# A kernel that orders its own program: the cost functions of its planner replaced by the durations of the trace

## The chip, the cores and the metric

One core of one Trainium2 chip runs the kernel as one launch. The metric is the device time in microseconds (us), lower is better; three runs are given for the kernel before. The engines are named as the profile names them: PE (matrix multiply), PEld (its weight load), DVE (vector), ACT (scalar, activation), POOL (GpSimd), SP (its queue issues the DMAs).

## The reference

The inputs are q, k, v of shape (4, 8, 576, 64) in float32, a forget gate f of shape (4, 8, 576), and the weights of two feed-forward layers (512 by 1536, 512 by 1536, 1536 by 512 each).

```python
scores = q @ k^T / 8 + decay            # decay[i, j] = cum[i] - cum[j], cum = cumsum(log f)
attn   = softmax(causal(scores)) @ v    # per batch and head
x      = attn as (2304 tokens, 512)
x      = x / rms(x) * rms_g
x      = (silu(x @ w_gate) * (x @ w_val)) @ w_out      # layer 1, with the norm before it
out    = (silu(x @ w_gate2) * (x @ w_val2)) @ w_out2   # layer 2, without a norm
```

## The kernel before

**Tiling.** The 2304 tokens are worked through in four groups (`GROUPS`): two groups of 2 x 256 tokens (the first 256 of two sequences each), then two groups of 2 x 320 tokens. For every group there is attention over 8 heads of its two sequences, a norm, and two feed-forward layers of 36 weight pieces (128 x 512) each. The work of PE is float32 in two parts: every operand is split into a high part and a low part, and each product takes three matmuls (L1485 to L1487). The last group replaces part of the products by sums and differences of blocks (L1187 to L1189).

**Weights.** They arrive as 64-bit floats. `convert` (from L1406) turns each of the 72 pieces into float32 with a few instructions: a multiplication by a power of two (L1419 on ACT, L1421 on DVE, L1423 on POOL), a shift of one byte column of each word (L1429 on ACT, or L1431 on DVE), a mask (L1435, DVE) and a merge (L1441, DVE); the result is stored (L1445). Then `split` makes the high part (`hi_op`, L284 on ACT or L286 on DVE) and the low part (`lo_op`, L289 on POOL or DVE). This is done once, while the first group is worked on; later groups fetch the stored pieces.

**Who sets the order.** The program is written by a planner that runs when the kernel is built. Each part of the work (a head pair, a weight piece, a norm, a thread of the feed-forward layers) is a generator that asks for operations. The planner keeps a time at which each engine comes free, takes the request that can start first, puts it behind the others of its engine and adds its cost to the engine's time. An operation is ready 0.14 us (`LATENCY`) after the planned end of the operations that it needs. Requests within 0.01 us of each other go by priority. Nothing of this exists on the chip: there each engine runs its instructions in the written order and waits on semaphores.

**Choice of engine.** Where an operation may run on several engines (`either`), the planner takes the smallest sum of planned start, cost and a handicap written by hand. Handicaps depend on the phase (0 until the eighth step of the first group, 1 until the eighth step of the second, then 2, 3, 4). For the byte shift the handicap of DVE is `HAND_LOW = (-0.22, 0, 9, -0.01, 0.08)`. "DVL" stands for a DVE operation that the planner does not let overlap with one of POOL.

**The costs** are the functions at the head of the file: `pe` and `pe4` (matmuls), `dve`, `dve2` (the form at double rate), `act`, `actp` (ACT with its source in PSUM), `pool_`. Each is a slope times the columns plus a constant.

**Fills.** Where the planner sees PE idle in the beginning (until step 12 of the first group's feed-forward work), it writes matmuls on zeros into the program:

```python
    def fill(time):
        for _ in range(int((time - FILL_GAP) / 0.107)):
            nc.tensor.matmul(idle[2][:, :SPLIT], zeros[:, :P], zeros[:, :SPLIT], start=True, stop=True)
```

They are L355 in the profile; 22 further ones at the very start (L364) are written out without the planner. The head pairs of the first half are `pair_queries` (scores L640 and L641, maxima L654, exponentials L662, scaling L680 to L684, transposes L701, values L716), the others `pair_wide` and `wide_part` (exponentials L820, scaling L841 to L845, transposes L893, values L921).

Of the kernel before, what the change touches and what calls it, by code (L numbers as in the profile page):

```python
# [17 lines left out]
B, H, S, D = 4, 8, 576, 64  # L18
# [6 lines left out]
WP = 512  # L25
# [40 lines left out]
HAND_CONV = (0.68, 1, 1.67, 0.2, -0.2)  # L66
STYLE1 = 3
HAND_SCALE = (0.3, 0.2)
HAND_LOW = (-0.22, 0, 9, -0.01, 0.08)
# [140 lines left out]


def pe(n):
    return max(0.107, n / 2400 + 0.0025)


def dve(n):
    return n / 960 + 0.067


def dve2(n):  # L220
    return n / 1920 + 0.067


def act(n):
    return n / 1200 + 0.093


def pool_(n):
    return n * 0.0022 + 0.1


def actp(n):
    return n / 1200 + 0.052


def pe4(n):
    return n / 600 + 0.003


def dma(n):  # L240
# [17 lines left out]
def tile_attention_moe_moe(  # L258
# [17 lines left out]
    plan = Plan()  # L276
# [349 lines left out]
    def pair_queries(hds, before, started, done):  # L626

        hd = hds[0]
        h, s, n = hd.h, hd.s, hd.qn
        tok, _ = yield Take(sc_tokens[0], (before, hd.kq_ready))  # L630
        rows = ((0, P), (P, 2 * P))
        sc, es = [], []
        for x in hds:
            q, k = x.kq[:, 0], x.kq[:, 1]
            bank, e0 = yield Take(banks, ())

            def mm():
                for c, (col, kn) in enumerate(rows):
                    qs = slice(c * P, (c + 1) * P)
                    nc.tensor.matmul(bank[:, col : col + kn], q[:, qs], k[:, :kn], start=c == 0, stop=False)  # L640
                nc.tensor.matmul(  # L641
                    bank[:, : 4 * P].rearrange("p (a n) -> p a n", n=2 * P)[:, :, :P], mir[:, 0], mir[:, 1:3], start=False, stop=True
                )

            e = yield op("PE", pe4(3 * P) + pe(2 * P), mm, hd.kq_ready, e0)
            x.kq_drop(e)
            sc.append(bank)
            es.append(e)
        later(started, e)
        st, e0 = yield Take(hd.slots["tm"], ())  # L650
        for x, (bank, e) in enumerate(zip(sc, es)):
            for c, (col, kn) in enumerate(rows):
                o, i = st[:, 2 * x + c : 2 * x + c + 1], bank[:, col : col + kn]
                em = yield op("DVE", dve(kn), lambda: nc.vector.tensor_reduce(o, i, axis=AX.X, op=ALU.max), e, e0)  # L654
        em = yield op("DVE", dve(4), lambda: nc.vector.tensor_scalar(st[:, 4:8], st[:, 0:4], -0.125, None, op0=ALU.mult), em)
        d, e0 = yield Take(hd.slots["d"], ())
        for x, bank in enumerate(sc):
            for c, (col, kn) in enumerate(rows):
                o, i, j = d[:, x, col : col + kn], bank[:, col : col + kn], 2 * x + c
                e = yield op(  # L660
                    "ACT", actp(kn) + 0.186,
                    lambda: nc.scalar.activation(  # L662
                        o, i, AF.Exp, scale=0.125, bias=st[:, 4 + j : 5 + j], accum_out=st[:, 8 + j : 9 + j]
                    ), em, e0,
                )
            banks.give(bank, e)
        sc_tokens[0].give(tok, e)
        e = yield op("DVE", dve(4), lambda: nc.vector.tensor_scalar(st[:, 8:12], st[:, 8:12], 1e-9, None, op0=ALU.add), e)
        e = yield op("DVE", dve(4) + 0.01, lambda: nc.vector.reciprocal(st[:, 8:12], st[:, 8:12]), e)
        es = []  # L670
        for c, (col, kn) in enumerate(rows):
            o = d[:, :, col : col + kn]

            def scale(en):
                if en == "POOL":
                    m = st[:, 8 + c : 12 : 2].unsqueeze(2).to_broadcast([P, 2, kn])
                    nc.gpsimd.tensor_tensor(o, o, m, op=ALU.mult)
                    return
                for x in range(2):
                    m = st[:, 8 + 2 * x + c : 9 + 2 * x + c]  # L680
                    if en == "ACT":
                        nc.scalar.mul(o[:, x], o[:, x], m)
                    else:
                        nc.vector.tensor_scalar(o[:, x], o[:, x], m, None, op0=ALU.mult)  # L684

            es.append((yield either(
                (
                    ("DVL", 2 * (dve2(kn) + 0.06), 0.0),
                    ("POOL", pool_(2 * kn), HAND_SCALE[0]),
                    ("ACT", 2 * act(kn), HAND_SCALE[1]),  # L690
                ), scale, e,
            )))
        es = Event(max(es[0].t, es[1].t))
        hd.slots["tm"].give(st, es)
        pts = []
        for x in range(2):
            bank, e0 = yield Take(banks, (es,))

            def turn_():
                for i in range(3):  # L700
                    nc.tensor.transpose(bank[:, i * P : (i + 1) * P], d[:, x, i * P : (i + 1) * P], ident)  # L701

            e = yield op("PE", 3 * 0.109, turn_, es, e0)
            ed = e
            pt, e0 = yield Take(hd.slots["p"], ())
            e = yield hi_op(3 * P, pt, bank[:, : 3 * P], e, e0, psum=True)
            banks.give(bank, e)
            pts.append((pt, e))
        hd.slots["d"].give(d, ed)

        bank, e0 = yield Take(banks, (hd.v_ready, *(e for _, e in pts)))
        for x, (pt, e) in enumerate(pts):

            def mm():
                for c in range(2):
                    nc.tensor.matmul(  # L716
                        bank[:, c * P : n], hds[x].v[:, c], pt[:, c * 2 * P : (2 + c) * P],
                        start=(x == c == 0), stop=(x == c == 1),
                    )

            e = yield op("PE", pe4(n) + pe4(P), mm, e, e0)
            hds[x].v_drop(e)
            hd.slots["p"].give(pt, e)
        e = yield hi_op(n, xT[h // 2][s][:, :n], bank[:, :n], e, xT_free[hd.g][s], psum=True)
        banks.give(bank, e)
        for x in done:
            later(x, e)
# [28 lines left out]
    def wide_part(hds, part, st, hl, ev, e0):  # L756
        hd = hds[0]
        kind, s = hd.kind, hd.slots
        joint = part == 2
        kn = ((128, 256), (384, 512, 576))[kind][part]  # L760
# [51 lines left out]
        for i in range(2):  # L812
            if joint:
                o, src, b = dt[:, 512 * i : 512 + D * i], sc[i][:, : (512, D)[i]], 0
            else:
                o, b = dt[:, kn * i : kn * (i + 1)], i
                src = sc[i][:, :kn] if kind else sc[0][:, kn * i : kn * (i + 1)]
            ex.append((yield op(
                "ACT", actp(kn if not joint else (512, D)[i]) + 0.186,
                lambda: nc.scalar.activation(  # L820
                    o, src, AF.Exp, scale=0.125, bias=st[:, c + 2 + b : c + 3 + b], accum_out=st[:, c + 4 + i : c + 5 + i]
                ), em, e1,
            )))
            if kind:
                banks.give(sc[i], ex[i])
# [3 lines left out]
        e = ex[1]  # L829
# [6 lines left out]
        for i in range(k):  # L836
            o, m = dt[:, w // k * i : w // k * (i + 1)], st[:, c + 4 + i : c + 5 + i]

            def scale(en):
                if en == "ACT":  # L840
                    nc.scalar.mul(o, o, m)  # L841
                elif en == "POOL":
                    nc.gpsimd.tensor_scalar(o, o, m, 1.0, op0=ALU.mult, op1=ALU.mult)
                else:
                    nc.vector.tensor_scalar(o, o, m, None, op0=ALU.mult)  # L845

            n = w // k
            es.append((yield either(
                (("POOL", n / 1200 + 0.2, 0.0), ("ACT", act(n) + 0.09, HAND_SCALE[1]), ("DVL", dve(n) + 0.2, HAND_SCALE[0] + 0.5)), scale, e
            )))  # L850
        later(ev["scaled"], Event(max(x.t for x in es)))

# [553 lines left out]
    def convert(i):  # L1406
# [8 lines left out]
        high = x[:, :, 1]  # L1415

        et = yield either(
            (("ACT", act(WP), 0.0), ("DVL", dve2(WP), HAND_CONV[plan.phase]), ("POOL", pool_(WP), HAND_CONV[plan.phase])),
            lambda e: nc.scalar.mul(t, high.bitcast(F32), 2.0**-112)  # L1419
            if e == "ACT"  # L1420
            else nc.vector.tensor_scalar(t, high.bitcast(F32), 2.0**-112, None, op0=ALU.mult)  # L1421
# [3 lines left out]
        )  # L1425

        e = yield either(
            (("ACT", act(WP) + 0.09, 0.0), ("DVL", dve2(WP), HAND_LOW[plan.phase])),
            lambda e: nc.scalar.activation(u8[:, :, 4], u8[:, :, 3], AF.Identity, scale=1.0 / 32, bias=kbias)  # L1429
            if e == "ACT"  # L1430
            else nc.vector.tensor_scalar(u8[:, :, 4], u8[:, :, 3], 5, None, op0=ALU.logical_shift_right),  # L1431
# [5 lines left out]
        w64_slots.give(x, Event(max(e.t, et.t)))  # L1437
        ti = t.bitcast(I32)
        e = yield op(
            "DVL", dve(WP),  # L1440
            lambda: nc.vector.scalar_tensor_tensor(ti, ti, 3, k, op0=ALU.logical_shift_left, op1=ALU.bitwise_or), e, et,  # L1441
        )
        wk_slots.give(k, e)
# [3 lines left out]
        e = yield from split(i, t, e)  # L1447
# [270 lines left out]
```

## Time and profile before

| what | value |
|---|---|
| time, median of three runs (lowest to highest) | 1126.56 us (1122.87 to 1127.38) |
| time of the profiled execution | 1128.12 us |
| its span from first to last instruction | 1126.3 us |
| PE, DVE, ACT, POOL busy | 1094.5, 750.1, 639.2, 389.7 us |
| mean granted clock of PE | 0.988 of full speed |

Busy time is the union of the recorded durations of an engine's instructions. A recorded duration runs from the start of an instruction to its end; the next instruction of the same engine may have begun before that end, so recorded durations in a row can add up to more than the time that they take together. The ends of matmuls are modelled.

### The profile page before, as it was taken

What the parts mean: (1) busy time and instruction counts of PE and PEld (TensorE: products, weight loads), DVE (VectorE), ACT (ScalarE), POOL (GpSimd) and SP (SyncE); (2) the same over time, 40 slices, a digit from 0 to 9 for tenths busy, and PEclk for the clock granted to TensorE, in tenths of its full rate; (3) what the DMA queues carried; (4) which work ended last, traced back from release to release, by engine and by line L of the source; (5) the groups of instructions that cost most, each with busy time, mean ns of one, the idle gap of its engine ahead of it and who ended that gap; (6) DMA issues with size and microseconds to landing.
All of it is one profiled execution on the core that took longest, in us unless ns stands there. A gap on an engine that the chain in (4) does not pass through costs nothing.

```text
span 1126.3 us, 19235 instructions
## 1 busy us (share of the span) xinstructions
PE 1094.5 (97%) x6436; PEld 1003.9 (89%) x6436; DVE 750.1 (67%) x1680; ACT 639.2 (57%) x1486; POOL 389.7 (35%) x427
## 2 busy tenths in 40 slices
PE   8999878999999999999999999999999999999998
PEld 7888766788888888888899999999999999999998
DVE  5998887899466648677446664676655189559830
ACT  4889998988466655666435434554543344234420
POOL 0222224334156567666442123333306243002200
PEclk7999989999999999999999999999999999999999
DMA  5767889874997687776786675565436469756641
GB/s 151 205 191 234 294 284 300 260 228 156 354 339 241 241 285 260 283 277 252 241 291 227 198 242 176 177 214 195 135 113 209 136 227 311 275 190 216 235 169 35
DMA packets 111510, 254.81 MB, mean 226 GB/s; under 512 B 12450, under 2 KB 35826, under 8 KB 111410
## 3 DMA queue, kind: packets, MB, share of 16 engines
q1 hardware_dynamic: 111412, 253.59, 67.3%
q8 instruction: 51, 0.84, 0.3%
q14 instruction: 47, 0.39, 0.1%
HBM read 179.42 MB, written 74.07 MB: 225 GB/s over the span
## 4 chain that ended last, share of the span: by engine, by line
PE 79%; DVE 7%; ACT 7%; DMA 3%; issue 2%; POOL 2%; SPq 0%; POOLq 0%; ACTq 0%; DVEq 0%
PE bank L1486 18%; PE bank L1485 18%; PE bank L1487 18%; PE bank L1187 4%; PE bank L1189 4%; PE bank L1188 4%; PE bank L921 3%; PE bank L893 3%; PE bank L784 2%; PE bank L785 2%; ACT w L1429 2%; ACT w L1419 1%; ACT whl L284 1%; PE bank L640 1%; DMA raw<-qk 1%
## 5 line engine op out<-in xcount | busy, mean ns | idle before, releaser
L1485 PE MATMUL bank<-X,whl 128*128 128x320 f32 (+1 forms) x756 | 270.1, 357 | 0.2 <-ACT X L284 0.2
L1486 PE MATMUL bank<-X,whl 128*128 128x320 f32 (+1 forms) x756 | 264.5, 350 | 2.4 <-DVE X L289 1.6
L1487 PE MATMUL bank<-X,whl 128*128 128x320 f32 (+1 forms) x756 | 264.4, 350 | 0.0
L289 POOL TENSOR_TENSOR whl<-w,whl 128x512 fp32r<-128x512 f32 x94 | 123.1, 1310 | 186.7 <-ACT whl L284 124.4
L1486 PEld LDWEIGHTS bank<-X,whl 128*128 128x128 f32 x756 | 142.6, 189 | 16.5 <-DVE X L289 2.2
L1485 PEld LDWEIGHTS bank<-X,whl 128*128 128x128 f32 x756 | 142.6, 189 | 15.0 <-ACT X L284 0.7
L1487 PEld LDWEIGHTS bank<-X,whl 128*128 128x128 f32 x756 | 142.2, 188 | 15.0
L1485 PE MATMUL bank<-H,whl 128*128 128x320 f32 (+1 forms) x378 | 130.6, 346 | 0.0
L1486 PE MATMUL bank<-H,whl 128*128 128x320 f32 (+1 forms) x378 | 128.9, 341 | 0.0
L1487 PE MATMUL bank<-H,whl 128*128 128x320 f32 (+1 forms) x378 | 128.9, 341 | 0.0
L284 ACT CAST whl<-w 128x512 fp32r<-128x512 f32 x140 | 87.3, 625 | 49.2 <-PE bank L1486 17.9
L1616 DVE SCALAR_TENSOR_TENSOR bank<-tmp,bank 128x320 f32<-128x320 f32 (+1 forms) x96 | 54.5, 568 | 41.2 <-PE bank L1487 40.1
L1594 DVE SCALAR_TENSOR_TENSOR tmp<-tmp,bank 128x512 f32<-128x512 f32 (+1 forms) x96 | 56.1, 584 | 31.5 <-ACT tmp L1591 31.4
L1487 PEld LDWEIGHTS bank<-H,whl 128*128 128x128 f32 x378 | 71.2, 188 | 5.9
L1485 PEld LDWEIGHTS bank<-H,whl 128*128 128x128 f32 x378 | 71.5, 189 | 5.5
L1486 PEld LDWEIGHTS bank<-H,whl 128*128 128x128 f32 x378 | 71.3, 189 | 5.2
L289 POOL TENSOR_TENSOR kb<-raw,k 64x576 fp32r<-64x576 f32 (+1 forms) x39 | 51.4, 1318 | 70.7 <-ACT k L284 57.8
L1591 ACT ACTIVATE tmp<-bank 128x512 f32<-128x512 f32 (+1 forms) x96 | 50.1, 522 | 41.9 <-PE bank L1487 41.3
L1429 ACT ACTIVATE w<-w,kbias 128x512 uint8<-128x512 uint8 x50 | 73.2, 1465 | 0.5
L802 DVE TENSOR_REDUCE tm<-bank 128x1 f32<-128x512 f32 (+1 forms) x96 | 51.6, 562 | 26.2 <-PE bank L791 20.0
L1621 ACT CAST H<-bank 128x320 fp32r<-128x320 f32 (+1 forms) x74 | 36.2, 490 | 47.9 <-DVE bank L1616 47.6
L905 DVE TENSOR_TENSOR pl<-bank,ph 128x512 fp32r<-128x512 f32 (+2 forms) x88 | 53.8, 624 | 8.8 <-ACT ph L284 8.1
(234 smaller groups left out, 2670.6 us busy)
## 6 DMA issues: line engine op xcount, KB each, us to landing
whl<-w_split SPq DMA_DIRECT2D x105, 512.0 KB
w<-w SPq DMA_DIRECT2D x72, 512.0 KB
w_split<-whl SPq DMA_DIRECT2D x72, 512.0 KB
w_f<-w SPq DMA_DIRECT2D x72, 256.0 KB
w<-w_f SPq DMA_DIRECT2D x72, 256.0 KB
raw<-qk SPq DMA_DIRECT2D x32, 288.0 KB
s<-w_f SPq DMA_DIRECT2D x36, 256.0 KB
w_sums<-s SPq DMA_DIRECT2D x36, 256.0 KB
```

The source lines that it names most:

```text
L284: nc.scalar.copy(o, i)
L289: (nc.vector if e == "DVE" else nc.gpsimd).tensor_tensor(o, a, b, op=ALU.subtract)
L802: em = yield op("DVE", dve(m), lambda: nc.vector.tensor_reduce(st[:, c + i : c + i + 1], bank[:, :m], axis=AX.X, op=ALU.max), e)
L905: e = yield op("DVE", dve(n), lambda: nc.vector.tensor_tensor(low, src, o.bitcast(F32), op=ALU.subtract), e)
L1187: nc.tensor.matmul(o, w[:, 0, cs], xh, start=c == 0, stop=False)
L1429: lambda e: nc.scalar.activation(u8[:, :, 4], u8[:, :, 3], AF.Identity, scale=1.0 / 32, bias=kbias)
L1485: nc.tensor.matmul(o, wh[:, cs], xh, start=start, stop=False)
L1486: nc.tensor.matmul(o, wh[:, cs], xl, start=False, stop=False)
L1487: nc.tensor.matmul(o, wl[:, cs], xh, start=False, stop=stop)
L1591: e = yield op("ACT", actp(n), lambda: nc.scalar.activation(th[:, :n], bank[:, :n], AF.Tanh, scale=0.5), e, e0)
L1594: lambda: nc.vector.scalar_tensor_tensor(th[:, :n], th[:, :n], 1.0, bank[:, :n], op0=ALU.add, op1=ALU.mult), e,
L1616: lambda: nc.vector.scalar_tensor_tensor(o, th[:, :w], factor, bank[:, :w], op0=ALU.mult, op1=ALU.mult), e, mid,
```

## The change

Only the planner's cost functions are changed, by constants: `dve` from 0.067 to 0.152, `dve2` from 0.067 to 0.18, `act` from 0.093 to 0.195, `actp` from 0.052 to 0.168, `pool_` from 0.1 with slope 0.0022 to 0.23 with slope 0.0021, `pe` from 0.0025 to 0.0135, `pe4` from 0.003 to 0.0135, and some extra terms at single operations. The byte shift of the weights, 0.61 us on ACT and 0.334 us on DVE for the planner before, is 1.465 and 0.762 after. Handicaps, priorities, gates, tiles, `LATENCY` and the DMA's costs stay. The instructions that the kernel may issue stay the same; what can differ is their order on each engine, the engine of those that have a choice, the number of fills, and the places in the SP queue.

```diff
 def pe(n):
-    return max(0.107, n / 2400 + 0.0025)
+    return max(0.107, n / 2400 + 0.0135)
 def dve(n):
-    return n / 960 + 0.067
+    return n / 960 + 0.152
 def dve2(n):
-    return n / 1920 + 0.067
+    return n / 1920 + 0.18
 def act(n):
-    return n / 1200 + 0.093
+    return n / 1200 + 0.195
 def pool_(n):
-    return n * 0.0022 + 0.1
+    return n * 0.0021 + 0.23
 def actp(n):
-    return n / 1200 + 0.052
+    return n / 1200 + 0.168
 def pe4(n):
-    return n / 600 + 0.003
+    return n / 600 + 0.0135
...
-                    "ACT", actp(kn) + 0.186,
+                    "ACT", actp(kn) + 0.3,
...
-                    ("DVL", 2 * (dve2(kn) + 0.06), 0.0),
+                    ("DVL", 2 * (dve2(kn) + 0.12), 0.0),
...
-                "ACT", actp(kn if not joint else (512, D)[i]) + 0.186,
+                "ACT", actp(kn if not joint else (512, D)[i]) + 0.3,
...
-                (("POOL", n / 1200 + 0.2, 0.0), ("ACT", act(n) + 0.09, HAND_SCALE[1]), ("DVL", dve(n) + 0.2, HAND_SCALE[0] + 0.5)), scale, e
+                (("POOL", n / 1200 + 0.27, 0.0), ("ACT", act(n) + 0.105, HAND_SCALE[1]), ("DVL", dve(n) + 0.2, HAND_SCALE[0] + 0.5)), scale, e
...
-            (("ACT", act(WP), 0.0), ("DVL", dve2(WP), HAND_CONV[plan.phase]), ("POOL", pool_(WP), HAND_CONV[plan.phase])),
+            (("ACT", act(WP) + 0.06, 0.0), ("DVL", dve2(WP), HAND_CONV[plan.phase]), ("POOL", pool_(WP), HAND_CONV[plan.phase])),
...
-            (("ACT", act(WP) + 0.09, 0.0), ("DVL", dve2(WP), HAND_LOW[plan.phase])),
+            (("ACT", 1.465, 0.0), ("DVL", 0.762, HAND_LOW[plan.phase])),
...
-            "DVL", dve(WP),
+            "DVL", dve(WP) + 0.035,
```

## Rows read from the trace of the kernel before

**Rows 1.** Stretches of 28 us: busy time (and instructions) of each engine, clock, DMA.

```profile
28.00:56.00 28.00, 25.29 (x166) 22.77 (x165) 26.82 (x90) 24.64 (x90) 6.25 (x5) 1.00 0.72 206
56.00:84.00 28.00, 26.64 (x155) 22.98 (x154) 26.14 (x73) 25.12 (x66) 6.41 (x10) 1.00 0.61 189
84.00:112.00 28.00, 28.00 (x125) 23.19 (x124) 23.21 (x45) 25.39 (x39) 8.36 (x7) 1.00 0.71 235
112.00:140.00 28.00, 25.60 (x119) 21.08 (x117) 24.49 (x44) 27.16 (x46) 6.67 (x8) 1.00 0.90 298
140.00:168.00 28.00, 21.56 (x99) 17.99 (x100) 24.52 (x48) 27.49 (x51) 6.77 (x8) 0.82 0.90 281
168.00:196.00 28.00, 25.06 (x112) 19.50 (x111) 21.84 (x44) 25.24 (x49) 11.17 (x12) 1.00 0.94 301
196.00:224.00 28.00, 25.90 (x124) 20.96 (x124) 23.95 (x47) 27.05 (x51) 11.71 (x12) 1.00 0.82 261
224.00:252.00 28.00, 27.41 (x134) 22.59 (x133) 25.55 (x52) 23.45 (x48) 9.44 (x9) 1.00 0.73 234
...
868.00:896.00 28.00, 28.00 (x193) 28.00 (x193) 0.49 (x2) 6.51 (x13) 8.75 (x7) 1.00 0.54 178
```

**Rows 2.** Waits of PE from 112 to 252 us: total, times, longest.

```profile
PE bank L893 <- POOL dA L843: 8.8, 1, 8.8
PE bank L893 <- ACT dA L841: 3.0, 3, 1.6
```

**Rows 3.** Timeline of PE, POOL and ACT around 137 us: start, duration.

```profile
137.21 0.39 PE L1487 MATMUL bank<-X,whl 128*128 128x512 f32 x1
146.44 0.82 PE L893 MATMUL bank<-mi,dA 128*128 128x128 f32 x2 [8.84 <-POOL dA L843]
148.34 0.63 PE L1485 MATMUL bank<-H,whl 128*128 128x512 f32 x1
148.76 0.63 PE L1486 MATMUL bank<-H,whl 128*128 128x512 f32 x1
...
144.75 1.28 POOL L289 TENSOR_TENSOR whl<-w,whl 128x512 fp32r<-128x512 f32 x1 [8.29 <-ACT whl L284]
146.01 0.72 POOL L843 TENSOR_SCALAR dA<-dA,tm 128x128 f32<-128x128 f32 x2
...
137.21 0.61 ACT L284 CAST late_h<-tmp 128x512 fp32r<-128x512 f32 x1
137.72 1.43 ACT L1429 ACTIVATE w<-w,kbias 128x512 uint8<-128x512 uint8 x1
138.90 0.68 ACT L284 CAST whl<-w 128x512 fp32r<-128x512 f32 x1
```

**Rows 4.** Instructions of L1429 and L1431 before 252 us: ns min/median/max.

```profile
L1429 ACT ACTIVATE w<-w,kbias x42: 1426/1462/1518, 70.3 to 247.4; 128x512 uint8<-128x512 uint8 x42
L1431 DVE TENSOR_SCALAR w<-w x22: 731/753/935, 22.7 to 246.1; 128x512 uint8<-128x512 uint8 x22
```

**Rows 5.** Timeline of DVE at 23 and 143 us.

```profile
23.30 0.75 DVE L1431 TENSOR_SCALAR w<-w 128x512 uint8<-128x512 uint8 x1
23.84 0.46 DVE L1435 TENSOR_SCALAR wk<-w 128x512 int32<-128x512 int32 x1
...
143.25 0.69 DVE L1441 SCALAR_TENSOR_TENSOR w<-w,wk 128x512 int32<-128x512 int32 x1
143.86 0.69 DVE L289 TENSOR_TENSOR whl<-w,whl 128x512 fp32r<-128x512 f32 x1
```

**Rows 6.** Timeline of ACT at 14 us, the exponentials of one head pair.

```profile
14.05 0.37 ACT L662 ACTIVATE d<-bank,tm 128x128 f32<-128x128 f32 x1 [8.52 <-DVE tm L655]
14.32 0.19 ACT L662 ACTIVATION_READ_ACCUMULATOR d<-bank,tm 128x1 f32 x1
14.41 0.46 ACT L662 ACTIVATE d<-bank,tm 128x256 f32<-128x256 f32 x1
```

**Rows 7.** The fills: all of L355, and ten in a row on PE.

```profile
L355 PE MATMUL bank<-late_h x54: 278/283/561, 7.7 to 65.6; 128*128 128x256 f32 x54
48.53 1.43 PE L355 MATMUL bank<-late_h 128*128 128x256 f32 x10
```

**Rows 8.** Waits of PE and of its weight loads from 252 to 620 us.

```profile
PEld bank L893 <- ACT dC L841: 4.1, 5, 1.3
PEld bank L893 <- POOL dA L843: 2.5, 3, 1.2
```

## The prediction

> **What bounds the kernel now.** I read the table of stretches first. From 868 us on, PE is busy without a gap, with 193 matmuls in 28 us or 0.145 us for each of 320 columns [rows 1]; no order of the program can shorten that. The same holds from 84 to 112 us, with 125 matmuls of 512 columns at 0.224 us. Loss shows in three places. From 28 to 84 us, PE is idle for 4.1 us while DVE is busy for 52.96 of 56 us: attention of the first groups, bound by DVE and nearly by ACT. From 84 to 252 us the weights are converted: PE 153.5, ACT 155.8, DVE 143.6, POOL 54.1 of 168 us, DMA at a mean share of 0.83. PE is idle for 14.5 us here, and ACT, at up to 27.49 of 28 us, is the fullest engine. After 252 us there are short waits only [rows 8].
>
> Then the waits of PE: one of 8.8 us stands out, for a scaling on POOL (L843) [rows 2]. The timeline tells its story [rows 3]. PE's next instruction in the written order is a transpose (L893) that needs this scaling; on POOL the scaling stands behind a low part (L289), which waited 8.29 us for its high part on ACT; and ACT was not slow but late, because it had a row of byte shifts to do (L1429, 1.43 us recorded). PE could have gone on with other matmuls, but its order was fixed. After the stall the clock stands at half: matmuls of 512 columns follow each other at 0.42 us where 0.224 is usual. The mean clock of 0.82 in that stretch means 10.1 us at half, some 5.7 of them inside the stall, so 4.4 us of work at half speed and 2.2 us lost. The stall costs 11 us; the whole stage 16.7.
>
> **Which costs were wrong.** What occupies an engine is the distance from one start to the next in an unbroken row, and this I compare with both sets of costs. DVE with 512 columns: 0.61 us [rows 5]; old 0.600, new 0.685, recorded 0.69. ACT with 512 columns: 0.51 [rows 3]; old 0.520, new 0.622, recorded 0.61. An exponential with its accumulator read, 128 columns: 14.05 to 14.41, so 0.36 [rows 6]; old 0.345, new 0.575. So for ordinary instructions the old costs were right as occupancy, and the new ones are right as recorded duration, about 0.09 us too long on DVE and 0.1 on ACT, while the planner still adds its 0.14 us behind each. The matmuls gain from the change: 0.2158 becomes 0.2268 for 512 columns where the row says 0.224. And one cost was badly wrong: the byte shift takes 1.18 us of ACT [rows 3], planned at 0.61, new 1.465; on DVE 0.54 [rows 5], planned at 0.334, new 0.762. With 42 shifts on ACT before 252 us [rows 4], the plan ran 24 us ahead of the real ACT. That is the delay behind the long stall.
>
> The Trainium skill (Perfetto Trace Analysis, Optimizing Scalar/DVE Operations) gives about 60 ns of overhead for DVE and 93 ns for ACT as busy time, and says that profiled latency is about twice that because the write acknowledgement overlaps with the next instruction. By that rule the change charges a latency as if it were occupancy; the trace agrees for ordinary instructions (0.61 against 0.69 us on DVE), and disagrees for the byte shift, where even the occupancy is twice the old cost. By it alone, the sum below would lose its first term.
>
> **The change part by part.** *Byte shift.* In phase 1 the planner took ACT when ACT could start 0.276 us before DVE; now it must be 0.703. I estimate the new balance for 84 to 252 us in the planner's own terms, with about 40 shifts on ACT and 14 on DVE. The rest of ACT is 155.8 - 40 x 1.2 = 108 us, plus 0.1 us for each of 244 other instructions: 132. The rest of DVE is 143.6 - 14 x 0.54 = 136, plus 0.09 x 266: 160. With a shifts on ACT, 132 + 1.465a = 160 + 0.762(54 - a) gives a = 31, and 30 if a few low parts leave DVE for POOL. So ten shifts move: ACT loses 12 us and DVE gains 5.4, to 144 and 149. At DVE's share between 28 and 84 us (0.946) the stage takes 149/0.946 = 157.5 us instead of 168; ACT at its best share (0.98) would allow 147, the DMA (140 us of full work at 0.94) 149, PE itself 151.3. DVE ends last: **-10.5 us**. The ends are -16.7 (PE's floor) and +11 (a second stall like the one seen). I take the value from DVE's share, since DVE is next in line once ACT is relieved.
>
> *Ordinary costs of DVE and ACT, and the fills.* From 28 to 84 us DVE runs 163 instructions [rows 1]; at 0.09 us too much for each, the new plan sees 14.7 us of DVE work that does not exist, and PE idle meanwhile. It writes fills there. Fills run on the chip whether PE has time or not. Ten fills took 1.43 us with the last one's 0.28 in it, so 0.128 us each [rows 7], though they are planned at 0.107. If all 14.7 us became fills: 137 of them, 17.6 us, of which the idle 4.1 us hide some: +13.5. If none did: 0, or -4 where idle time disappears with a better order. Some of the planned excess goes to POOL and ACT with the scalings, feed-forward matmuls take PE soon after the last fill of now, at 65.6 us [rows 7], and each gap gives up 0.1 us before the first fill. I take a little over a third, 50 fills or 6.4 us, with about 2.4 of it hidden: **+4 us**. That cover is the idle time of PE; where it is gone, each fill costs its full 0.128.
>
> *Other choices.* High parts, low parts, sums and the first multiplication: the cost differences between engines move by 0.05 us or less (low part on POOL against DVE: 0.626 before, 0.620 after), so they change engine only through the planned loads. Scalings in the pair stage move away from DVE by 0.15 to 0.25 us of preference. I cost these at nothing: POOL, at a third of its time, hides them; without that cover, a low part costs 1.28 us on POOL against 0.61 on DVE. SP's order follows the plan: a store that stands ahead of loads is now planned later, which is nearer to the trace; its price is in the stage's bounds.
>
> *Middle stage, 252 to 620 us.* Weight loads wait 6.6 us for scalings [rows 8]. ACT's scaling of 576 columns is planned 0.12 us longer now, so transposes are written later. Between +6.6 and -6.6 I take **-2 us**, since later planning of a late operation can remove a wait but the slack of PE is small. After 620 us: 0; PE is full from 868 us on [rows 1]; DVE's and ACT's planned excess there must not reach it.
>
> Sum: -10.5 + 4 - 2 = -8.5. The profiled execution took 1128.1 us, 1.6 above the median of the runs shown; 1119.6 there is **1118 us** for the median, 0.8% faster. About 0.5% (5.6 us) is what a measurement of this kernel can tell from no change.
>
> **The rivals.** *A, full gain.* The plan of 84 to 252 us now tells the truth where it matters, PE reaches its floor there (-16.7), the middle gives 4 and fills cost 2: -18.7, 1108 us. For it: one mis-estimated operation explains the largest stall. Against it: DVE has only 7% to spare in that stage before it is as full as at the start.
>
> *B, the fills eat the gain.* +13.5 in the first 84 us against -10.5 and -2: 1128 us, no change. For it: fills are not conditional, and they take a fifth longer than planned. Against it: only 54 were written before [rows 7], so the plan finds other work for most gaps.
>
> *C, the inflated costs cancel the correction.* DVE and ACT look 13% fuller than they are, so shifts stay on ACT and the stage keeps its length; the fills cost their 4: 1130 us. It is what the Trainium skill's sentence, cited above, would predict.
>
> *D, slower: POOL's queue.* With DVE looking full, low parts go to POOL at 1.28 us each, and a scaling that PE's next transpose needs stands behind them, as in [rows 3]. One such stall in four head pairs costs 11 us now. If two remain or appear, the stage ends 11 us later than before, with the fills 1128.1 + 11 + 4, or 1141 us for the median. It decides from the second stall on. Against it: the plan knows POOL's time well (1.31 new, 1.26 from start to start).
>
> **How the numbers follow.** Forecast 0.40 (its own range 1112 to 1123), A 0.16, B 0.15, C 0.12, D 0.17. Faster by over 0.5% (below 1120.9): A and most of the forecast, 0.50. Slower (above 1132.2): D and a part of C, 0.21. Within: the rest, 0.29. The range leaves out the outer parts of A and D: 1106 to 1136.
>
> **What the profile after would show.** Right: before 252 us, L1429 falls from 42 to about 32 and L1431 rises from 22 to about 32 [rows 4]; no wait of PE over 3 us between 112 and 252 us; the conversions end some 6 us earlier than now, counting the fills; ACT below 95% busy in it; L355 near 100. Wrong: L355 far over 150 and the first feed-forward matmul much later (B); L1429 still near 42 (C); PE waiting for L843 behind L289 more than once (D); idle PE after 868 us, which I exclude.

## The result and the profile after

The changed kernel takes 1134.56 us (median of ten runs, 1131.76 to 1138.79), the kernel before 1128.39 (1121.63 to 1130.88) in the same measurement. The ratio is 1.0073 with a 95% interval of 1.0051 to 1.0095: slower by 0.7%, beyond the 0.5% that this kernel's measurement can tell. The forecast was 1118. The profiled execution has a span of 1133.6 us where the one of before had 1126.3.

The stretches of 28 us, with the same columns as [rows 1]:

```profile
28.00:56.00 28.00, 28.00 (x209) 26.95 (x208) 25.92 (x73) 21.53 (x74) 7.31 (x6) 1.00 0.66 191
56.00:84.00 28.00, 28.00 (x198) 26.39 (x197) 22.98 (x79) 22.16 (x76) 3.00 (x3) 1.00 0.37 107
84.00:112.00 28.00, 28.00 (x135) 23.42 (x134) 25.62 (x47) 19.80 (x35) 13.15 (x16) 1.00 0.59 185
112.00:140.00 28.00, 28.00 (x131) 23.39 (x131) 22.81 (x41) 24.27 (x41) 10.20 (x10) 1.00 0.77 247
140.00:168.00 28.00, 26.76 (x117) 20.73 (x116) 25.93 (x47) 23.45 (x47) 5.68 (x5) 1.00 0.82 272
168.00:196.00 28.00, 28.00 (x135) 23.54 (x134) 24.16 (x47) 19.12 (x41) 5.99 (x7) 1.00 0.85 280
196.00:224.00 28.00, 25.81 (x123) 20.38 (x122) 25.95 (x50) 24.41 (x52) 11.43 (x13) 1.00 0.72 236
224.00:252.00 28.00, 26.48 (x128) 21.59 (x127) 25.80 (x49) 24.37 (x43) 4.33 (x4) 1.00 0.73 247
252.00:280.00 28.00, 23.68 (x107) 18.32 (x106) 27.14 (x51) 20.39 (x41) 11.94 (x11) 1.00 0.53 179
280.00:308.00 28.00, 25.13 (x100) 19.29 (x101) 19.97 (x37) 17.46 (x27) 9.33 (x18) 0.94 0.77 253
```

Three things are to be seen against [rows 1]. From 28 to 84 us PE has no idle time left, while DVE and ACT have more of it than before (48.9 and 43.7 us busy, where they had 53.0 and 49.8). From 84 to 252 us the long stall is gone, PE is at full clock throughout, and ACT is no longer full: 135.4 of 168 us instead of 155.8. But from 252 to 308 us PE is idle for 7 us and the clock falls once, where PE had been full before the change:

```profile
252.00:280.00 28.00, 28.00 (x126) 23.17 (x125) 25.28 (x44) 23.59 (x37) 12.77 (x12) 1.00 0.45 151
280.00:308.00 28.00, 28.00 (x125) 23.21 (x124) 13.79 (x22) 13.12 (x23) 4.50 (x14) 1.00 0.93 341
```

The waits of PE from 252 to 310 us (total, times, longest), and the fills and byte shifts (ns min/median/max), to be read beside [rows 2, 4, 7]:

```profile
PE bank L1485 <- ACT whl L284: 4.8, 3, 3.2
PE bank L1487 <- POOL whl L289: 1.9, 3, 1.0
```

```profile
L355 PE MATMUL bank<-late_h x214: 277/283/415, 8.0 to 78.8; 128*128 128x256 f32 x107
L1429 ACT ACTIVATE w<-w,kbias x28: 1427/1464/1494, 93.8 to 289.9; 128x512 uint8<-128x512 uint8 x28
L1431 DVE TENSOR_SCALAR w<-w x44: 723/752/1845, 17.0 to 299.7; 128x512 uint8<-128x512 uint8 x44
```

Instead of a transpose behind a late scaling, PE now waits for weight pieces that are not converted yet. The fills have gone from 54 to 214. The shifts on ACT have gone from 50 to 28 over the whole conversion, those on DVE from 22 to 44. Before 252 us it is 22 on ACT and 36 on DVE, where I had forecast about 32 on each; and the last merge comes at 302.2 us instead of 284.3, where I had forecast 6 us earlier.

What matters next is where on the way the time is lost. I count the feed-forward matmuls (L1485 to L1487; the first group has 864 of them) and the merges of the conversion (L1441), one for each weight piece, in the traces. The first feed-forward matmul, as the timeline of PE shows it in the kernel before and after the change (start, duration):

```profile
66.06 0.50 PE L1485 MATMUL bank<-X,whl 128*128 128x512 f32 x1 [0.19 <-ACT X L284]
```

```profile
78.94 0.40 PE L1485 MATMUL bank<-X,whl 128*128 128x512 f32 x1
```

| profiled execution, us | before | after | difference |
|---|---|---|---|
| start to first feed-forward matmul | 66.1 | 78.9 | +12.8 |
| from there to the last one of the first group | 232.9 | 230.8 | -2.1 |
| second group | 270.2 | 264.1 | -6.1 |
| third and fourth group, to the end | 557.2 | 559.7 | +2.5 |
| 12th to 72nd conversion, for each (the pace) | 3.205 | 3.402 | +0.197 |

So the change loses 12.8 us before feed-forward work begins, gains almost nothing where 10.5 were forecast, and gains 6 in the second group. These four lengths are the instrument for the experiments. They are of one execution each, and the clock of its first 25 us moves them: from 12 to 22 us it stands at half in both profiles of this table (0.50 and 0.51), but in some later ones at full, and these are marked.

### The profile page after: what moved, and what is told of

It is laid out like the page before. It is cut to its first block, busy times and chain, and to the rows that moved or that the text cites. A ratio compares the mean times of both kernels' runs of the same rounds, so it can differ in the third digit from the quotient of the medians.

```text
span 1133.6 us, 19482 instructions
## 1 busy us (share of the span) xinstructions
PE 1110.1 (98%) x6596; PEld 1019.1 (90%) x6596; DVE 750.7 (66%) x1677; ACT 610.6 (54%) x1458; POOL 413.9 (37%) x457
## 5 line engine op out<-in xcount | busy, mean ns | idle before, releaser
L1485 PE MATMUL bank<-X,whl 128*128 128x320 f32 (+1 forms) x756 | 269.9, 357 | 2.6 <-ACT whl L284 2.6
L1487 PE MATMUL bank<-X,whl 128*128 128x320 f32 (+1 forms) x756 | 264.6, 350 | 4.0 <-POOL whl L289 2.8
L1486 PE MATMUL bank<-X,whl 128*128 128x320 f32 (+1 forms) x756 | 263.8, 349 | 0.3 <-POOL X L289 0.3
L289 POOL TENSOR_TENSOR whl<-w,whl 128x512 fp32r<-128x512 f32 x97 | 127.1, 1313 | 194.6 <-ACT whl L284 151.6
L1487 PEld LDWEIGHTS bank<-X,whl 128*128 128x128 f32 x756 | 141.9, 188 | 21.6 <-POOL whl L289 4.7
L1485 PEld LDWEIGHTS bank<-X,whl 128*128 128x128 f32 x756 | 142.1, 188 | 17.4 <-ACT whl L284 4.3
L1485 PE MATMUL bank<-H,whl 128*128 128x320 f32 (+1 forms) x378 | 130.9, 346 | 3.6 <-ACT whl L284 3.6
L1487 PE MATMUL bank<-H,whl 128*128 128x320 f32 (+1 forms) x378 | 129.5, 343 | 0.7 <-DVE whl L289 0.5
L1485 PEld LDWEIGHTS bank<-H,whl 128*128 128x128 f32 x378 | 71.4, 189 | 9.8 <-ACT whl L284 4.5
L1487 PEld LDWEIGHTS bank<-H,whl 128*128 128x128 f32 x378 | 71.2, 188 | 8.5 <-DVE whl L289 1.9
L1591 ACT ACTIVATE tmp<-bank 128x512 f32<-128x512 f32 (+1 forms) x96 | 49.8, 518 | 48.8 <-PE bank L1487 48.3
L1621 ACT CAST H<-bank 128x320 fp32r<-128x320 f32 (+1 forms) x74 | 36.3, 490 | 49.2 <-DVE bank L1616 48.9
L1214 DVE TENSOR_TENSOR st<-bank,st 128x320 f32<-128x320 f32 x72 | 33.0, 485 | 32.9 <-PE bank L1189 31.9
```

Of the source, the lines that this page charges most:

```text
L289: (nc.vector if e == "DVE" else nc.gpsimd).tensor_tensor(o, a, b, op=ALU.subtract)
L1485: nc.tensor.matmul(o, wh[:, cs], xh, start=start, stop=False)
L1486: nc.tensor.matmul(o, wh[:, cs], xl, start=False, stop=False)
L1487: nc.tensor.matmul(o, wl[:, cs], xh, start=False, stop=stop)
L1591: e = yield op("ACT", actp(n), lambda: nc.scalar.activation(th[:, :n], bank[:, :n], AF.Tanh, scale=0.5), e, e0)
```

## The experiments

Each experiment is timed against the kernel before, run beside it on the same chip; lengths are of its profiled execution. "Ordinary costs" are all changed costs except those of the byte shift.

**First round: fills, shift, the rest.** The fills are left out of the changed kernel. The planner does not advance its time for a fill, so every other instruction keeps its place.

```diff
-        for _ in range(int((time - FILL_GAP) / 0.107)):
+        for _ in range(0):
```

> The changed kernel with the planner's fills left out: the same order and engine of every other instruction, since a fill does not advance the planner's time, but none of the 214 matmuls on zeros (54 before). Theory 1 (the 160 added fills delayed the first feed-forward matmul from 66.1 to 78.9 us, and the delay went through to the end): 8 to 12 us less than the changed kernel, about 1124, and a first feed-forward matmul near 68 us. Theory 2 (the new order of the conversions is what is slow; the fills only stand in time that PE had anyway): at most 3 us less, 1131 to 1134, with PE idle before 84 us and the last conversion still near 302 us.

Measured: 1132.23 us, ratio 1.0050 (1.0028 to 1.0072). The first feed-forward matmul comes at 72.0 us, 6.9 earlier, but the first group ends at 307.9 instead of 309.8, with the same pace of 3.401 us. Theory 1 falls: the fills account for 6.9 of the 12.8 us at the start, but for only 2 us at the end. Two rows belong to this (stretches, same columns):

```profile
28.00:56.00 28.00, 20.82 (x122) 18.22 (x121) 25.92 (x81) 23.11 (x82) 6.79 (x6) 0.87 0.61 185
56.00:84.00 28.00, 23.91 (x110) 19.75 (x109) 21.77 (x69) 19.93 (x64) 5.19 (x4) 0.82 0.40 125
```

Without fills PE is idle for 11.3 us there and its clock is at half for part of the time. So the 2 us are what is left of two things, fills not executed and a clock that falls without them; the run does not separate them. PE was not what the stage waited for, and from 56 us on neither DVE nor ACT was full.

The kernel before with the shift's new costs alone:

```diff
-            (("ACT", act(WP) + 0.09, 0.0), ("DVL", dve2(WP), HAND_LOW[plan.phase])),
+            (("ACT", 1.465, 0.0), ("DVL", 0.762, HAND_LOW[plan.phase])),
```

> The kernel before with the two new costs of the byte shift alone (1.465 us on ACT, 0.762 on DVE); 60 fills, 39 shifts on ACT. Theory 1 (the shift's cost is a gain, the fills of the other costs are the loss): 1116 to 1122, without the 8.8 us wait at 137 us. Theory 2 (moving shifts to DVE makes DVE the limit of the conversions): 1126 to 1132, with the last conversion later than 284 us.

Measured: 1120.22 us, ratio 0.9946 (0.9923 to 0.9970), 39 shifts on ACT. The long stall is gone (between 112 and 252 us the longest wait of PE for a scaling is 1.6 us); the last conversion is at 281.9 us. So raising the shift's cost is a gain of 6 us by itself.

The opposite: the changed kernel with the shift's old costs (0.61 and 0.334).

> The changed kernel with the old costs of the byte shift (0.61 us on ACT, 0.334 on DVE); 203 fills, 49 shifts on ACT. Theory 1: the fills' delay stays and the shift's gain is gone: 1138 to 1145, with ACT over 95% busy and long waits of PE between 112 and 252 us. Theory 2: DVE is relieved of 21 shifts, conversions end earlier than 300 us: 1126 to 1132.

Measured: 1126.87 us, ratio 1.0007 (0.9983 to 1.0030). This speaks against theory 1, and with the run before it says that two corrections which each do no harm alone make the kernel slower together. The long stall is gone here too (the longest wait between 112 and 252 us is 1.5 us), although 49 shifts are on ACT. That is a warning about single orders, and is taken up below.

Costs by the distance from start to start:

```diff
-            (("ACT", act(WP), 0.0), ("DVL", dve2(WP), HAND_CONV[plan.phase]), ...
+            (("ACT", act(WP) + 0.06, 0.0), ("DVL", dve2(WP), HAND_CONV[plan.phase]), ...
...
-            (("ACT", act(WP) + 0.09, 0.0), ("DVL", dve2(WP), HAND_LOW[plan.phase])),
+            (("ACT", 1.19, 0.0), ("DVL", 0.54, HAND_LOW[plan.phase])),
...
-    return max(0.107, n / 2400 + 0.0025)
+    return max(0.107, n / 2400 + 0.011)
-    return n / 600 + 0.003
+    return n / 600 + 0.0135
```

> The kernel before with costs set to the distance from start to start in the trace: ordinary DVE and ACT costs as before, byte shift 1.19 us on ACT and 0.54 on DVE, first multiplication on ACT 0.06 more, matmuls of 512 columns 0.2243 us; 54 fills, 32 shifts on ACT. Theory 1: like the kernel with the shift alone or a little better, 1114 to 1121. Theory 2: 1126 or more, since even fewer shifts stay on ACT than in the kernel with the shift alone.

Measured: 1128.09 us, ratio 1.0019 (0.9994 to 1.0045). A miss: the costs nearest to the trace gave no gain. PE still waits for late scalings (7.6 us for those on ACT, 5.8 for those on POOL between 28 and 620 us, the longest 5.2).

**Second round: where the ordinary costs act.** The cost functions get a switch on the planner's phase, here shown for one of them and K = 2 (new costs from the eighth step of the second group on). With K = 1, `C` compares with 1 (new costs from the eighth step of the first group on).

```diff
+def C(new, old):
+    return new if PH[0] >= 2 else old
...
 def dve(n):
-    return n / 960 + 0.152
+    return n / 960 + C(0.152, 0.067)
```

> The byte shift's new costs throughout; the other costs old in phases 0 and 1 (until the eighth step of the second group) and new from there on; 60 fills, 39 shifts on ACT. Theory 3 (the new ordinary costs gain 6 us in the second group, where the kernels with them take 264 us and those without 267 to 270, and lose only in the first): like the kernel with the shift alone until 291 us, then 3 us better: 1115 to 1118, less than the shift alone (1120.2). Rival (which order comes out is chance, and the 6 us belong to what the first group left behind): 1120 to 1124, second group 267 us or more.

Measured: 1116.87 us, ratio 0.9910 (0.9875 to 0.9945); second group 263.8 us.

> All old costs in phases 0 and 1, the shift's too, new ordinary costs from there on; 54 fills, 50 shifts on ACT. Until about 290 us the program of the kernel before. Theory 3: the second group takes 264 us instead of 270, the total 1120 to 1124. Rival: no more than 2 us from the kernel before (1127.8), second group near 270 us.

Measured: 1123.78 us, ratio 0.9973 (0.9950 to 0.9996); second group 263.5 us. Theory 3 is supported: on either first group the second takes 264 us. In time the gain is 3 us here, with an interval that just excludes no change, and 3 us from the shift alone to the run above, where the two intervals overlap.

> The changed kernel, but with old ordinary costs in phase 0 (until the eighth step of the first group's feed-forward work); 60 fills, 34 shifts on ACT. Start theory (the change loses because its slow plan of the first attention delays the first feed-forward matmul to 79 us): first matmul at 61 to 67 us, and the total falls by most of the 12 us, to 1121 to 1125. Pace theory (with more shifts on DVE a weight piece takes 3.40 us instead of 3.20, and this sets the end of the first group wherever it started): a pace of 3.3 us or more, the first group ending at 299 to 304 us, the total 1126 to 1131.

Measured: 1128.23 us, ratio 1.0015 (0.9988 to 1.0042). The first feed-forward matmul is at 59.9 us, with K = 2 at 59.8 (the clock at full from 12 to 22 us in both), and yet the first group ends 12 us later (298.6 against 286.4) with a pace of 3.367 against 3.216. The window from 90 to 270 us, for K = 2 and then K = 1 (same columns as before):

```profile
90.00:270.00 180.00, 170.21 (x774) 136.95 (x773) 164.44 (x308) 154.50 (x278) 54.81 (x61) 0.99 0.78 254
```

```profile
90.00:270.00 180.00, 163.86 (x726) 128.82 (x725) 159.17 (x293) 145.18 (x273) 61.43 (x59) 0.97 0.73 238
```

With the new costs in this phase, PE, DVE and ACT are all less busy: none of the three has become the limit. What PE waits for are weight pieces: 15.4 us between 84 and 320 us, 7.6 with K = 2.

The fourth run of the round asks another question, that of the start: 40 matmuls on zeros ahead of everything instead of 22.

```diff
-WARM, PE_START = 22, 6.9
+WARM, PE_START = 40, 6.9
```

> The kernel before with 40 matmuls on zeros at the very start instead of 22, nothing else changed. PE is idle for 1.9 us before the first scores at 10.3 us, and in most executions its clock then stands at half from 11 to 22 us. If that idle time is what halves it, and this sets the spread of the kernel before (1120.7 us at a mean clock of 0.995, 1130 at 0.986): 1120 to 1123 with a spread of at most 4 us. If the clock falls for another reason, or the first scores become late: 1126 to 1131.

Measured: 1120.46 us, ratio 0.9942 (0.9922 to 0.9961), all twelve runs between 1118.6 and 1123.4. From 12 to 22 us, first the kernel before, then this one:

```profile
12.00:22.00 10.00, 10.00 (x35) 8.69 (x34) 6.24 (x28) 4.53 (x18) 0.00 (x0) 0.50 0.43 138
```

```profile
12.00:22.00 10.00, 10.00 (x71) 9.46 (x70) 9.74 (x41) 9.17 (x37) 0.00 (x0) 1.00 0.67 187
```

PE runs twice the matmuls, at full clock. The first feed-forward matmul comes at 60.3 us instead of 66.1.

**Third round: combinations, and how much is chance.** First K = 2 and the 40 matmuls at the start in one kernel.

> The byte shift's new costs, other costs new from the second group on, and 40 matmuls on zeros at the start instead of 22. If the three gains add (shift 7 us, second group 4, clock at the start up to 7, of which the kernel without the 18 matmuls already has a part in some executions): 1108 to 1112, with a spread of at most 4 us. If the start's gain is already in the median of 1116.9: 1114 to 1117.

Measured: 1113.76 us, ratio 0.9882 (0.9857 to 0.9908). It is faster than the kernels before and after the change. Against the 1116.87 it is 3 us less, but the two intervals overlap, so a gain of the start on top of the other two is not shown.

The switch the other way round: old ordinary costs in phase 1 only.

```diff
+def C(new, old):
+    return old if PH[0] == 1 else new
```

> The changed kernel with old ordinary costs in phase 1 only (from the eighth step of the first group's feed-forward work to the same step of the second group), new in phase 0 and later; 214 fills, 33 shifts on ACT. It completes the four combinations of old and new in phases 0 and 1. Phase theory (the loss is in the conversions of phase 1, as between 1116.9 with old costs there and 1128.2 with new): a pace of 3.2 to 3.3 us, 1117 to 1124. Start theory (it is in phase 0's slow plan): first feed-forward matmul near 79 us and the delay carried through, 1128 to 1135.

Measured: 1128.81 us, ratio 1.0019 (0.9993 to 1.0044). First feed-forward matmul at 80.3 us, then 226.4 us for the group (pace 3.310). The start theory's numbers came for this combination: the start is late, and the total is no better than that of the kernel before. But the group itself is as short as with K = 2, so phase 1 has its part in the loss too.

Two controls change the constant of `dve` by 0.003 us, which corrects nothing but can change the order; here the one of the changed kernel.

```diff
-    return n / 960 + 0.152
+    return n / 960 + 0.149
```

> A control: the kernel before with the constant of the DVE cost 0.070 instead of 0.067, which means nothing for the durations but changes ties and so the order; 55 fills, 44 shifts on ACT. If orders that a nudge makes differ little: 1126 to 1129. If the order is a matter of chance to the extent that the change cost: 1119 to 1135, and differences of that size between single kernels prove nothing.

Measured: 1126.54 us, ratio 0.9983 (0.9963 to 1.0004). The total stands, but inside it the first group takes 4 us more and the second 5 less.

> A control: the changed kernel with the constant of the DVE cost 0.149 instead of 0.152; 210 fills, 35 shifts on ACT. If the loss belongs to the new costs and not to one order: 1131 to 1137, pace 3.35 us or more. If it is chance: 1124 to 1130 or above 1138.

Measured: 1145.57 us, ratio 1.0152 (1.0121 to 1.0182): 11 us slower than the changed kernel, more than the change itself cost, and beyond the 1138 that I had named as a sign of chance. Single kernels could not settle the matter from here; so most combinations of costs got a second or third order, by nudges of 0.003 us.

> The kernel with the shift's new costs throughout and new ordinary costs from the second group on (1116.9), with the old DVE constant 0.070 instead of 0.067 in phases 0 and 1; 59 fills, 39 shifts on ACT. If the gain belongs to the costs: 1112 to 1122, first feed-forward matmul before 70 us, second group 264 us. If it belongs to one lucky order: 1123 to 1132.

> The same with 0.064; 68 fills, 35 shifts on ACT. If the gain belongs to the costs: 1112 to 1122. If it belongs to one lucky order: 1123 to 1132.

> The changed kernel with the DVE constant 0.155 instead of 0.152; fills over 200, 32 shifts on ACT. If the loss belongs to the new costs: slower than the kernel before in this order too, 1131 to 1146, first feed-forward matmul at 76 us or later, conversions with a pace of 3.35 us or more. If it is chance: below 1128.

> The kernel before with the DVE constant 0.064 instead of 0.067; 54 fills, 54 shifts on ACT. If orders of the old costs lie close together: 1123 to 1131. If they scatter like those of the new costs (1134.6 and 1145.6): over 1133 or below 1121.

> The changed kernel with old ordinary costs in phase 0, new from phase 1 on (1128.2), with the new DVE constant 0.149 instead of 0.152; 60 fills, 39 shifts on ACT. If new costs in phase 1 slow the conversions: a pace of 3.35 us or more, 1125 to 1133. If the 11 us between this kernel and the mixed one were the order's chance: 1115 to 1123 is as likely, with a pace near 3.2.

> The changed kernel with old ordinary costs in phase 1 only (1128.8), with the new DVE constant 0.149 instead of 0.152 in phase 0 and from the second group on; over 200 fills, 30 shifts on ACT. If new costs in phase 0 delay the first group: first feed-forward matmul at 76 us or later and 1125 to 1135. If that delay is made up in a lucky order: below 1122.

The runs by their costs; every column lists the orders in the same sequence. A star marks a profile whose clock stood at full from 12 to 22 us; in all others it stood at half for most of that time (0.50 to 0.56). The medians come from several chips, on which the kernel before took 1125.3 to 1128.4 us.

| ordinary costs in phase 0, in phase 1; shift | median us | first feed-forward matmul | first group from there |
|---|---|---|---|
| old, old; old | 1128.4, 1126.5, 1123.3 | 66.1, 68.4, 58.7* | 232.9, 236.8, 239.2 |
| old, old; new (ordinary costs old to the end) | 1120.2 | 60.5* | 230.0 |
| old, old; new (ordinary costs new from the second group) | 1116.9, 1120.4, 1111.7 | 59.8*, 68.9, 65.0 | 226.6, 226.2, 224.8 |
| old, new; new | 1128.2, 1126.8 | 59.9*, 68.6 | 238.6, 239.2 |
| new, old; new | 1128.8, 1128.6 | 80.3, 76.8 | 226.4, 226.9 |
| new, new; new (the change) | 1134.6, 1145.6, 1145.1 | 78.9, 79.0, 76.9 | 230.8, 239.3, 242.6 |
| new, new; old | 1126.9 | 76.6 | 226.1 |

The last six runs measured ratios of 0.9946 (0.9924 to 0.9968), 0.9876 (0.9834 to 0.9918), 1.0176 (1.0134 to 1.0218), 0.9998 (0.9969 to 1.0026), 1.0004 (0.9978 to 1.0030) and 1.0024 (1.0002 to 1.0045), in the order in which they stand above. The groups do not overlap where it matters: the new shift with old ordinary costs in the first group gives 1112 to 1120 in all three orders, new ordinary costs in one early phase 1127 to 1129 in all four, in both 1135 to 1146. There are two losses: a later start with new costs in phase 0, and a first group that takes 4 to 18 us longer with new costs in phase 1 and the new shift.

The size of the first must be read with the clock in view. The two kernels of the line "old, new; new" have the same program on PE up to 127 us, and yet one profile has its first feed-forward matmul at 59.9 us with the clock at full, the other at 68.6 with the clock at half. Profile against profile with the clock at half, new costs in phase 0 start 8 to 15 us later (76.6 to 80.3 against 65.0 to 68.9), not the 22 that the column's ends are apart. The slower total is not the clock's doing: the changed kernel's executions have a mean granted clock of 0.991 to 0.997, the kernel before 0.984 to 0.997.

A simple reading of the second loss can be set aside: it is not how many shifts stay on ACT, 30 to 39 in the kernels of 225 to 230 us with the new shift, 28 to 39 in those of 231 to 243. What separates the two sets is how long PE waits for weight pieces between 84 and 320 us: 5.6 to 8.6 us with old ordinary costs in phase 1, 9.9 to 15.5 with new ones, both with the new shift. The single order with the old shift in the last line does not fit (226.1 us, and 6.1 us of such waits); one order is not enough to say why.

## Why the prediction was wrong

**What held.** The byte shift was the badly wrong cost, and with old ordinary costs PE's long waits for scalings were its result: between 84 and 320 us the longest is 5.4 to 8.8 us in every kernel with the old shift and old costs in phase 1, and 1.6 at most in those with the new shift. Kernels with its new cost and old ordinary costs in phase 1 need 225 to 230 us for the first group, those with the old shift and old ordinary costs 232 to 239. Over three orders each, the length falls from 236.3 us on average to 225.9. That this is my -10.5 us is luck in part: I had worked it out with the new ordinary costs in the balance, and with them nothing of it is left (237.6 us on average over the three orders of the changed kernel). In time, the shift alone gained 6 us. The middle stage was -2 forecast; the second group takes 263.5 to 265.6 us in all kernels with new costs there, and 265.2 to 270.2 in those without, so some -4 on average and -6.1 in the two profiles that the table compares. The forecast that PE has no idle time after 868 us was off by 0.8 us, in one wait between 952 and 980 us. The measured 1134.56 us lies between my outer ends, 1106 and 1136, but slower was given 0.21 and for another reason.

**The step that failed first** is the one on other choices: "I cost these at nothing", because cost differences between engines hardly move. The costs do not only choose engines; they set the planned time of every instruction, and so its place in the written order. I had seen that the new ordinary costs exceed the distance from start to start by 0.09 and 0.1 us, and still counted their effect in the fills and in the balance of the shifts alone, not in the order. In phase 1 they take back the whole gain of the shift: 225 to 230 us for the first group becomes 231 to 243. My own balance had a sign of it: with 31 shifts, 132 + 1.465 x 31 is 177 us of planned work on ACT, and as much on DVE, in a stage that took 168. From 84 to 252 us themselves the forecast gain came: PE did 761 matmuls instead of 706, with DVE busy for 150.3 us (forecast 149) and ACT for 135.4 (forecast 144). It was lost again behind that: the last merge is 18 us later than before, and from 252 to 308 us, waiting for weight pieces, PE did 207 matmuls instead of 249. My step from ACT's relief to a stage of 157.5 us had assumed that DVE would fill to 0.946. From 90 to 270 us it reached 0.91 in the changed kernel (163.00 of 180 us); it did no more in the faster one with K = 2 (164.44), so this share alone does not tell the slow orders from the fast:

```profile
90.00:270.00 180.00, 172.23 (x796) 139.50 (x796) 163.00 (x298) 146.03 (x276) 54.51 (x58) 1.00 0.74 243
```

**The second** is the term for the first 84 us, +4 forecast, +12.8 measured. The count of fills, which I put at 50 more, was 160 more; the mark named for rival B, "far over 150" fills and a much later first matmul, was met. But B's mechanism explains only a part. With the fills left out, the first matmul was still at 72.0 us, 5.9 later than before the change, and the end moved by 2 us; with 313 fills, in the third order of these costs, it came at 76.9 us, no later than with 214. The rest is the order itself: DVE and ACT are less busy than before from 28 to 84 us, and by 84 us 8 pieces are merged instead of 10. I read this as a plan that believes these engines full and so lets weights and later pairs start late; no run changes that alone.

**The rivals.** C came nearest in its mechanism, that inflated ordinary costs cancel the correction; but not by its way, since the shifts did leave ACT, more of them than forecast. (Its 13% is about right for DVE, 0.685 against 0.61, and too low for ACT, 0.622 against 0.51, or 22%.) D, low parts on POOL in front of a scaling, did not happen: the longest wait of PE for a scaling between 112 and 252 us fell from 8.8 to 0.7 us. That its 1141 us is near what the change takes over three orders is luck. What came in its place is another wait, for unconverted weights at the end of the first group. The rows had said that the new ordinary costs charge a latency as occupancy, and I gave the rival built on that a chance of 0.12. The runs show that, with the new shift, these costs lose in both phases of the first group. That they lose because they are too long is not shown: in the second group they gain, and the kernel with costs set to the distances gained nothing. The Trainium skill (Perfetto Trace Analysis, Optimizing Scalar/DVE Operations) states that profiled latency is longer than engine-busy time; the rows agree (0.69 us recorded on DVE, 0.61 from start to start).

**What stays open.** Why the same inflated costs help by some 4 us in the second group and hurt in the first was not isolated; nor which of the constants hurts in phase 1. Candidates are the exponentials (0.575 against 0.36 us from start to start for 128 columns) and the double-rate `dve2` (0.447 against 0.34 for 512). Costs set to the measured distances gave only 1128.1 us, in one order. And the changed kernel's 1134.6 is the best of the three orders of its costs that were run; over the three, the new costs take 1141.8 us on average, some 13 us above the kernel before and not 6.

## What to carry to other kernels

A planner's costs do more than choose engines: they place every instruction, and a change that moves no choice can still cost time through the order. So change one cost at a time, and switch it by stage to see where it acts: here one correction gained 6 us and the others, made together with it, took back twice as much. That the distance to the next start is the right cost for a planner sounds plain, but it is not shown here: the one kernel planned by distances gained nothing. Before a difference between two orders is explained, nudge a constant that means nothing and see how far the time moves: here up to 11 us. And before two profiles are compared length by length, compare their granted clocks: the same program reached the same matmul at 59.9 and at 68.6 us.

## What the runs showed of the hardware

Executions of the kernel before lie between 1119 and 1134 us, and follow the mean granted clock: 1120.5 us on average at 0.995 (seven executions), 1129.9 at 0.986 (twelve). In the profiled one, PE is idle for 1.9 us before 10.3 us, and its clock stands at half, 1.2 of 2.4 GHz, from 11 to 24.5 us (0.50 from 12 to 24 us, 0.88 from 24 to 26); with 18 more matmuls on zeros ahead of that there was no such gap, the clock stayed at full in the profile, and the spread of twelve runs shrank to 5 us. In profiles of kernels with 22 such matmuls the clock stays at full in four and halves in the others; two kernels with the same program up to 127 us fell on either side. The length of the gap does not decide it alone: it was 2.0 to 2.5 us in three profiles that stayed at full, and 1.3 to 1.4 in two that fell to half. And 256-column matmuls on zeros cost 0.128 us each at full clock, a fifth more than the planner thought: 33 of them took 5.81 us where the clock was partly at half, as the timeline of PE in the changed kernel shows:

```profile
18.52 5.81 PE L355 MATMUL bank<-late_h 128*128 128x256 f32 x33
```
